# Loading both token pairs ahead of the value weights in a gated linear-attention and MLP kernel, with new engine orders

## The chip, the cores and the metric

The kernel runs on one core of a Trainium2 chip (trn2). The metric is device time in microseconds (us) of one execution. A core has five engines that each work through their own list of instructions: TensorE (PE in the profile, with its weight loads listed as PEld), VectorE (DVE), ScalarE (ACT), GpSimd (POOL) and SyncE (SP), which here only issues DMAs. ScalarE issues the stores of the output.

## The reference

Inputs are 2048 tokens `x` of 512 bf16 values, and weights in bf16. Two branches are computed and mixed by a gate for each token:

```python
g = sigmoid((x * gate_w).sum(-1, keepdims=True))
# branch a: linear attention with 32 heads of 16
q, k, v = split(x @ wqkv)                       # wqkv is 512 x 1536
pq, pk = q @ w_phi[h], k @ w_phi[h]             # 16 x 16 for each head
phi = concat([softmax(p), softmax(-p)])         # of pq and of pk, 32 features a head
kv = sum over tokens of phi_k (x) v;   z = sum over tokens of phi_k
a = ((phi_q @ kv) / (phi_q @ z + 1e-6)) @ wo
# branch b: MLP
b = relu(x @ w1) @ w2                           # 512 -> 1376 -> 512
out = g * a + (1 - g) * b
```

The sums `kv` and `z` run over all tokens, so no output of branch a can be formed before the key features of the last token tile are in them.

## The kernel before

Tokens are handled in 16 tiles of 128 (index m) and in 4 chunks of 512 (index c). The program is a graph of named tasks. Each task has an engine, a function that emits its instructions and a list of tasks it depends on. The order of the tasks on each engine is not found at run time: it is written out in the table `ORDER`, one list of names for each engine (lines 17 to 63). An engine works strictly in that order and, ahead of a task, waits on semaphores for those of its dependencies that lie on other engines or are DMAs. The numbers `dur` and `lat` in the task definitions are planning figures; they emit nothing.

The tasks that matter here, with the lines of the profile:

- `xa0`, `xa1` (L265): DMAs on SP's queue that bring the first 512 tokens into `XN` (part of the buffer `FT`), two tiles in each. A partition receives two neighbouring rows from each DMA, 2 KB in one piece.
- `wva`, `wvb` (L265): the value weights, two halves of 256 rows, 1 KB a row. `w1a`, `w1b`, `w1c` bring `w1`, `wphi` the 16 x 16 matrices, `wkT` and `wqT` (L269) the key and query weights by transposing DMA, `x1` to `x3` the other three chunks of tokens, transposed by DMA.
- `xt0a` to `xt3b` (L325): the "turns", which transpose the first four token tiles on TensorE, two 128 x 128 blocks in each task (a and b). `xe00` to `xe31` move the results into `XT`, the a half on ScalarE (L337), the b half on VectorE (L339).
- `warm0`, `warm1` (L251): matmuls on constants at the start.
- `v0a` to `v3b` (L374): the values of the first four tiles, in half tasks of two matmuls; half a needs `wva`, half b `wvb`. `v4` to `v15` are whole, four matmuls. `ve0` to `ve15` (L379, ScalarE) move them to `VS`.
- `f1_j` and `f0_j` (L356): the fold of the key and query weights with the 16 x 16 matrices, laid out as block-diagonal `WBD` (`wbd0` to `wbd3`, VectorE, L309, made from `wphi`). `fe1_0`, `fe1_2` (VectorE, L319), `fe1_1`, `fe1_3` (ScalarE, L317) move the folded key weights to `WP`.
- `pr_k0` to `pr_k8`, `pr_q0` to `pr_q8` (L454): projections with the folded weights, two tiles a task (the last two tasks of each kind one tile). They share PSUM banks 0 and 1, so each waits for the eviction (`ev_`, L479, ScalarE) of the one before.
- The features of a projection, for each J in k0 to q8: `mx_J`, `mn_J` (VectorE, L483, L485: maximum and minimum of each head), `t1_J`, `t2_J` (GpSimd, L492: the subtractions), `ex_J` (ScalarE, L497), `sm_J` and `rc_J` (VectorE), `nm_J` (GpSimd, L506 for k, L529 for q: the normalisation).
- `kv0` to `kv15` (L513): the sums of key features by values. `kn`, `kz` (VectorE) take the sums out of PSUM behind `kv15`, and `nd` (L556), the numerators and denominators, need these.
- `h c_k` (L397) and `hr c` (L405): the MLP's first layer, `rl` (L415) its ReLU; three PSUM banks in turn. `b m` (L577) the second layer, `a m` (L583) the output projection into the same bank, `oe m` (L628) the gated eviction and `st m` (L631) the store. `gt` and `gv` fold the gate's weight into `w1`.

The first tasks in the lists before, of SP and of TensorE:

```python
"sp": "xa0 wva xa1 wvb w1a wphi wkT w1b x1 gw w1c wqT x2 x3 w2a w2b ..."
"pe": "warm0 xt0a xt0b xt1a xt1b v0a v1a xt2a xt2b xt3a xt3b warm1 v2a v3a v0b v1b v2b v3b h0_0 f1_0 f1_1 f1_2 "
      "f1_3 h0_1 pr_k0 h0_3 h0_2 pr_k1 h0_6 h0_4 pr_k2 h0_5 h0_7 pr_k3 ..."
```

Of the kernel before, what the change touches and what calls it, by code (L numbers as in the profile page):

```python
# [18 lines left out]
        "xa0 wva xa1 wvb w1a wphi wkT w1b x1 gw w1c wqT x2 x3 w2a w2b ht1 wo ht0 tq1 tq0 tq2 tq3 to0 to1 ht2 to2 "  # L19
        "tq4 tq5 to3 tq6 tq7 to4 to5 ht3 tq8 tq9 to6 to7 tq11 tq10 to8 to9 tq12 tq13 to11 to10 tq14 tq15 to12 "  # L20
# [18 lines left out]
    ),  # L39
    "dve": (  # L40
# [10 lines left out]
    ),  # L51
# [91 lines left out]
def bass_gated_mix__linear_kernel_hedgehog__dense_activation_relu__prompt_kernel(  # L143
# [11 lines left out]
    x2 = A_x.rearrange("b s d -> (b s) d")  # L155
    o2 = out.rearrange("b s d -> (b s) d")
    S, D = x2.shape
# [23 lines left out]
    with ExitStack() as es:  # L181
# [67 lines left out]
        def pe_warm(q, sizes):  # L249
            for n in sizes:  # L250
                last = q.matmul(PS[:, 5, 0:n], ONE[:, 0:P], ONE[:, 0:n], start=True, stop=True)  # L251
            return last

        add("warm0", "pe", lambda q: pe_warm(q, (D, D, D, D, D, D, P)), (), dur=1.36)
        add("warm1", "pe", lambda q: pe_warm(q, (2 * P,)), (), dur=0.108)
# [21 lines left out]
        def pair(i):  # L277
            return x2[2 * i * P:2 * (i + 1) * P, :].rearrange("(p t) d -> p (t d)", t=2)

        load("xa0", "sp", XN[:, 0:2, :].rearrange("p t d -> p (t d)"), pair(0), dur=0.47, lat=2.25)  # L280
        load("wva", "sp", WV[:, 0:2, :], wvr[:, 0:2, :], dur=0.46, lat=2.55)
        load("xa1", "sp", XN[:, 2:4, :].rearrange("p t d -> p (t d)"), pair(1), dur=0.5, lat=3.2)
        load("wvb", "sp", WV[:, 2:4, :], wvr[:, 2:4, :], dur=0.48, lat=3.75)
        load("w1a", "sp", W1[:, :, 0:512], w1r[:, :, 0:512], dur=0.51, lat=4.75)
        load("wphi", "sp", WPS[:, :, :], A_w_phi.rearrange("(g hl) r c -> (hl r) g c", g=ND), dur=0.55, lat=4.4)
        load_t("wkT", WT[:, ND:2 * ND, :], A_wqkv[:, D:2 * D], (), 4.1, 2.1)
# [61 lines left out]
        def rows(m):  # L348
            if m < 4:
                i = m // 2  # L350
                return o2[2 * i * P:2 * (i + 1) * P, :].rearrange("(p t) d -> p t d", t=2)[:, m % 2, :]
            return o2[m * P:(m + 1) * P, :]
# [30 lines left out]
        for m in range(4):  # L383
            for n, js in enumerate(((0, 1), (2, 3))):
                add(f"v{m}{'ab'[n]}", "pe", lambda q, m=m, js=js: pe_v(q, m, js, VB[m]),
                    (f"xe{m}{n}", f"wv{'ab'[n]}", *(("warm1",) if m == 3 else ()), *((f"v{m}a",) if n else ())), dur=0.44)
            evict_v(m, VB[m], (f"v{m}b",))
# [246 lines left out]
        for line in (("warm0", "xt0a", "xt0b", "xt1a", "xt1b", "v0a", "v1a", "xt2a", "xt2b", "xt3a", "xt3b", "warm1",  # L634
                      "v2a", "v3a", "v0b", "v1b", "v2b", "v3b", "h0_0"),
                     ("xe00", "xe10", "xe20", "xe30", "ve0"),
                     ("ident", "xe01", "xe11", "xe21", "xe31", "shift", "blk", "row4", "mk", "wbd0"),
                     ("iota_r", "iota_i", "iota_c", "gwz", "pads", "ones")):
            for a, b in zip(line, line[1:]):
                g.follow(a, b)  # L640
# [39 lines left out]
```

## Time and profile before

| | us |
|---|---|
| median of 3 runs (151.42 to 151.90) | 151.71 |
| the profiled execution | 151.17 |
| its span, first to last instruction | 149.2 |
| TensorE busy | 144.9 |
| VectorE busy | 110.8 |
| GpSimd busy | 109.7 |
| ScalarE busy | 91.1 |

The profile shows one execution. Its span leaves out 1.97 us that lie around the first and last instruction. Busy times are of matmuls, vector operations and so on; waiting and issuing of DMAs are not counted. Where a line of the profile gives a start and a length, both are in us from the start of the span; "[0.50 <-DMA WT...]" behind a line is the idle time of that engine just before, and what ended it. In the rows of DMA traffic, "under 2 KB" counts all packets smaller than that, those under 512 B included.

### The profile page before, as it was taken

Reading aid. Unit: us, or ns where it says so; the run is one execution under the profiler, and the core shown is the slowest. Engines: PE = TensorE matmul, PEld = TensorE weight load, DVE = VectorE, ACT = ScalarE, POOL = GpSimd, SP = SyncE. Lnnn points to the kernel's source line nnn. Section 1 sums busy time; section 2 is a strip of 40 time slices with the busy share of each in tenths; the row PEclk is TensorE's granted clock in tenths of the full one; section 3 lists DMA queues with packets and bytes.
Section 4 is the critical chain, followed back from the end, with each engine's and each line's share of the span. In section 5 each row is a group of like instructions: output and inputs, shape, how many; then the busy total and the mean of one; then the engine's idle time right before and its main releaser. Section 6 shows DMA issues by size and latency. Waiting matters only on the chain.

```text
span 149.2 us, 2538 instructions
## 1 busy us (share of the span) xinstructions
PE 144.9 (97%) x968; PEld 73.0 (49%) x984; DVE 110.8 (74%) x169; ACT 91.1 (61%) x127; POOL 109.7 (74%) x73
## 2 busy tenths in 40 slices
PE   7899999999999999999999999999999999999994
PEld 2454444454454645444547445444545454544553
DVE  0542679999995499989569899999979987817501
ACT  3347769997886888966896854476535443303131
POOL 4000599999999999999999999999958795060000
PEclk9999999999999999999999999999999999999999
DMA  5999999500003400000000061847495964787423
GB/s 140 295 199 223 259 166 276 191 0 0 4 2 94 116 7 0 0 0 0 4 0 0 0 141 32 151 104 186 102 172 109 245 156 107 135 208 211 106 73 108
DMA packets 45524, 16.11 MB, mean 108 GB/s; under 512 B 39272, under 2 KB 45256, under 8 KB 45512
## 3 DMA queue, kind: packets, MB, share of 16 engines
q1 hardware_dynamic: 43208, 13.89, 42.3%
q10 hardware_dynamic: 2304, 2.06, 4.3%
q8 instruction: 8, 0.13, 0.4%
q14 instruction: 4, 0.03, 0.1%
HBM read 4.41 MB, written 2.10 MB: 44 GB/s over the span
## 4 chain that ended last, share of the span: by engine, by line
PE 94%; DMA 3%; issue 1%; SPq 1%; DVE 0%
PE PS L577 24%; PE PS L397 23%; PE PS L454 19%; PE PS L374 9%; PE PS L583 9%; PE PS L513 3%; DMA FT<-in_A_x_dram 3%; PE PS L556 3%; PE PS L405 2%; PE PS L598 2%; PE PS L356 1%; PE PS L609 1%; SPq L265 1%; PE PS L325 0%; DVE OSB L619 0%
## 5 line engine op out<-in xcount | busy, mean ns | idle before, releaser
L492 POOL TENSOR_TENSOR TS<-PB,MX 128x1024 bf16<-128x1024 bf16 (+1 forms) x18 | 30.8, 1716 | 13.9 <-DVE MX L483 13.9
L499 DVE TENSOR_REDUCE ZB<-FT 128x128 f32<-128x2048 bf16 (+1 forms) x18 | 36.6, 2037 | 4.6 <-ACT FT L497 4.5
L397 PE MATMUL PS<-XT,W 128*128 128x512 bf16 x155 | 37.7, 379 | 0.3
L577 PE MATMUL PS<-W,HT 128*128 128x512 bf16 (+1 forms) x161 | 37.0, 379 | 0.2
L497 ACT ACTIVATE FT<-TS 128x2048 bf16<-128x2048 bf16 (+1 forms) x18 | 31.0, 1720 | 4.5 <-PE PS L513 2.4
L492 POOL TENSOR_TENSOR TS<-MN,PB 128x1024 bf16<-128x1024 bf16 (+1 forms) x18 | 30.8, 1720 | 0.1
L454 PE MATMUL PS<-WP,XT 128*128 128x512 bf16 x126 | 30.1, 379 | 0.1
L506 POOL TENSOR_TENSOR FT<-FT,SC 128x2048 bf16<-128x2048 bf16 (+1 forms) x9 | 29.5, 3285 | 0.0
L415 ACT ACTIVATE HT<-PS 128x512 bf16<-128x512 f32 x40 | 22.8, 601 | 6.3 <-PE PS L397 6.2
L628 ACT ACTIVATE OSB<-PS,OMG 128x512 bf16<-128x512 f32 x15 | 10.2, 685 | 23.5 <-PE PS L583 23.5
L479 ACT ACTIVATE PB<-PS 128x1024 bf16<-128x1024 f32 (+1 forms) x18 | 16.8, 932 | 12.3 <-PE PS L454 8.1
L577 PEld LDWEIGHTS PS<-W,HT 128*128 128x128 bf16 (+1 forms) x165 | 15.5, 97 | 17.4 <-ACT OSB L628 0.3
L397 PEld LDWEIGHTS PS<-XT,W 128*128 128x128 bf16 x160 | 15.0, 98 | 17.5 <-ACT HT L415 1.0
L483 DVE TENSOR_REDUCE MX<-PB 128x64 bf16<-128x1024 bf16 (+1 forms) x18 | 19.5, 1082 | 5.4 <-ACT PB L479 5.4
L485 DVE TENSOR_REDUCE MN<-PB 128x64 bf16<-128x1024 bf16 (+1 forms) x18 | 19.2, 1075 | 0.3 <-ACT PB L479 0.2
L454 PEld LDWEIGHTS PS<-WP,XT 128*128 128x128 bf16 x128 | 12.1, 98 | 14.0 <-DVE WP L319 0.4
L529 POOL TENSOR_TENSOR FT<-FT,SR 128x1024 bf16<-128x1024 bf16 (+1 forms) x9 | 15.6, 1736 | 0.6
L374 PE MATMUL PS<-WV,XT 128*128 128x512 bf16 x61 | 15.5, 379 | 0.2
L583 PE MATMUL PS<-WO,OT 128*128 128x512 bf16 x58 | 14.4, 378 | 0.1
L564 DVE SCALAR_TENSOR_TENSOR OTM<-PS,EG,RD 128x256 bf16<-128x256 f32 x32 | 14.1, 466 | 0.4
L562 DVE RECIPROCAL RD<-PS 128x16 f32<-128x16 f32 x32 | 7.0, 238 | 8.2 <-PE PS L556 7.9
L379 ACT ACTIVATE VS<-PS 128x512 bf16<-128x512 f32 x16 | 9.5, 607 | 3.0 <-PE PS L374 3.0
(54 smaller groups left out, 96.3 us busy)
## 6 DMA issues: line engine op xcount, KB each, us to landing
out_dram<-OSB ACTq DMA_DIRECT2D x15, 128.0 KB, 2.5
W<-in_B_w_dram SPq DMA_DIRECT2D x1, 1280.0 KB, 8.2
W<-in_B_w_dram SPq DMA_DIRECT2D x2, 512.0 KB, 5.0
FT<-in_A_x_dram SPq DMA_DIRECT2D x2, 256.0 KB, 3.4
WV<-in_A_wqkv_dram SPq DMA_DIRECT2D x2, 256.0 KB, 3.7
WO<-in_A_wo_dram SPq DMA_DIRECT2D x1, 512.0 KB, 4.6
W<-in_B_w_dram SPq DMA_DIRECT2D x1, 352.0 KB, 3.6
PHQ<-FT SPq DMA_TRANSPOSE x16, 2.8
```

What stands on the lines that cost most here:

```text
L374: last = q.matmul(PS[:, b, :], XT[:, j, m * P:(m + 1) * P], WV[:, j, :], start=(j == 0), stop=(j == ND - 1))
L397: last = q.matmul(PS[:, b, :], W1[:, j, k * P:(k + 1) * P], XT[:, j, chunk(c)], start=(j == 0), stop=(j == ND - 1))
L415: add(f"rl{a}_{k}", "act", lambda q, a=a, k=k, b=b: q.activation(HT[:, k, chunk(a)], PS[:, b, :], ACT.Relu), (f"h{a}_{k}",), dur=0.6)
L454: last = q.matmul(PS[:, n, :], XT[:, j, m * P:(m + 1) * P], WP[:, s, j, :], start=(j == 0), stop=(j == ND - 1))
L483: add(f"mx_{J}", "dve", lambda q, sl=sl, w=w, i=pbg: q.tensor_reduce(MX[:, sl, 0:w * H], i, AX.X, ALU.max), (f"ev_{J}", old("t1")), dur=0. ...
L485: add(f"mn_{J}", "dve", lambda q, sl=sl, w=w, i=pbg: q.tensor_reduce(MN[:, sl, 0:w * H], i, AX.X, ALU.min), (f"ev_{J}", old("t2")), dur=0. ...
L492: add(f"{tn}_{J}", "pool", lambda q, o3=o3, a3=a3, b3=b3: q.tensor_tensor(o3, a3, b3, ALU.subtract), (f"{'mx' if sg == 0 else 'mn'}_{J}", ...
L497: add(f"ex_{J}", "act", lambda q, fs=fs, ts=ts, w=w: q.activation(FT[:, fs, 0:w * F], TS[:, ts, 0:w * F], ACT.Exp), (f"t1_{J}", f"t2_{J}", ...
L499: add(f"sm_{J}", "dve", lambda q, fs=fs, sl=sl, w=w: q.tensor_reduce(ZB[:, sl, 0:2 * w * H], FT[:, fs, 0:w * F].rearrange("p (g d) -> p g ...
L506: add(f"nm_{J}", "pool", lambda q, f3=f3, sl=sl, w=w: q.tensor_tensor(f3, f3, SC[:, sl, 0:2 * w * H].unsqueeze(2).to_broadcast([P, 2 * w * ...
L577: last = q.matmul(PS[:, ab, :], HT[0:r, k, m * P:(m + 1) * P], W2[0:r, k, :], start=(k == 0), stop=False)
L583: last = q.matmul(PS[:, ab, :], OT[:, m % NOT, t, :], WO[:, t, :], start=False, stop=(t == ND - 1))
```

## The change

The DMAs of SP are put in the order xa0, xa1, wva, wvb. The first 512 tokens are laid out anew: a partition now holds four neighbouring rows, of which xa0 brings the first two and xa1 the other two, so that both read from the same 512 KB of `x` in pieces of 2 KB every 4 KB. The stores of tiles 0 to 3 follow this layout. `warm1` is taken out. On TensorE the written rule that binds the first tasks now asks only for the turns in order and then `h0_0`; the list itself has all turns but `xt3a` and `xt3b` ahead of the values. The lists of all engines are new; the set of tasks is the same but for `warm1`. In the changed kernel the lines below the table stand one to three higher (L265 is L264, L356 is L353).

```diff
     "sp": (
-        "xa0 wva xa1 wvb w1a wphi wkT w1b x1 gw w1c wqT x2 x3 w2a w2b ht1 wo ht0 tq1 tq0 tq2 tq3 to0 to1 ht2 to2 "
+        "xa0 xa1 wva wvb w1a wphi wkT w1b x1 gw w1c wqT x2 x3 w2a w2b ht0 ht1 wo tq1 tq0 ht2 tq2 tq3 to0 to1 tq4 "
...
     "pool": (
-        "iota_r iota_i iota_c gwz pads ones t1_k0 t2_k0 t1_k1 t2_k1 t1_k2 t2_k2 nm_k0 t1_k3 t2_k3 t2_k4 t1_k5 "
-        "t1_k4 nm_k2 nm_k1 t2_k5 t2_k6 t1_k6 nm_k3 t1_k8 t1_k7 t2_k7 t2_k8 nm_k4 t2_q0 t1_q0 nm_k5 t1_q1 t2_q1 "
-        "nm_k6 t1_q2 ra_q0 t2_q2 nm_q0 nm_k7 nm_k8 ra_q1 nm_q1 t1_q3 t2_q3 t1_q4 ra_q2 nm_q2 t2_q4 t2_q5 ra_q3 "
...
+        "iota_r iota_i iota_c gwz pads ones t1_k0 t2_k0 t1_k1 t2_k1 t2_k2 t1_k2 t2_k3 t1_k3 t1_k4 nm_k0 t2_k4 "
+        "nm_k1 t1_k5 t2_k5 nm_k2 t2_k7 t1_k6 t2_k6 t1_k7 nm_k3 t2_q0 t1_k8 nm_k4 t2_k8 t1_q0 nm_k5 nm_k6 t2_q1 "
+        "t1_q1 ra_q0 t2_q2 nm_q0 t1_q2 nm_k7 nm_k8 ra_q1 nm_q1 t1_q3 t2_q3 ra_q2 nm_q2 t1_q4 t2_q4 t1_q5 ra_q3 "
...
     "act": (
-        "xe00 xe10 xe20 xe30 ve1 ve2 ve3 fe1_1 fe1_3 ve0 rl0_0 ev_k0 rl0_3 rl0_1 rl0_2 ev_k1 rl0_6 rl0_4 ev_k2 "
-        "ex_k0 rl0_5 ev_k3 rl0_9 ex_k1 rl0_8 ev_k4 ex_k2 rl1_0 rl0_7 rl1_1 ev_k5 rr0 ve4 ex_k3 ev_k6 rl1_4 rl1_2 "
...
+        "xe00 xe10 xe20 xe30 ve1 ve2 rl0_0 fe1_1 fe1_3 rl0_3 rl0_1 ve0 ev_k0 ve3 rl0_6 ev_k1 rl0_2 ev_k2 ex_k0 "
+        "rl0_5 ev_k3 rl0_4 ex_k1 rl0_9 ev_k4 ve4 rl0_8 ex_k2 rl0_7 ev_k5 ve5 ex_k3 rl1_0 rl1_1 ve6 ev_k6 rl1_3 "
...
     "dve": (
-        "ident xe01 xe11 xe21 xe31 shift blk wbd3 wbd2 row4 mk wbd1 wbd0 fe1_0 fe1_2 mx_k0 mn_k0 mx_k1 mn_k1 "
-        "mx_k2 mn_k2 sm_k0 rc_k0 mx_k3 mn_k3 mx_k4 gv mn_k4 sm_k2 mx_k5 gr0 sm_k1 rc_k2 sm_k3 mx_k6 rc_k1 mn_k5 "
...
+        "ident xe01 xe11 xe21 xe31 shift blk row4 wbd2 wbd1 mk wbd3 wbd0 fe1_2 fe1_0 mx_k0 mn_k0 mx_k1 mn_k1 gv "
+        "mx_k2 mn_k2 sm_k0 mn_k3 mx_k3 mx_k4 mn_k4 rc_k0 sm_k2 sm_k1 mx_k5 rc_k1 mn_k6 gr0 rc_k2 mn_k5 sm_k3 "
...
     "pe": (
-        "warm0 xt0a xt0b xt1a xt1b v0a v1a xt2a xt2b xt3a xt3b warm1 v2a v3a v0b v1b v2b v3b h0_0 f1_0 f1_1 f1_2 "
-        "f1_3 h0_1 pr_k0 h0_3 h0_2 pr_k1 h0_6 h0_4 pr_k2 h0_5 h0_7 pr_k3 h0_9 h0_8 pr_k4 h1_1 h1_0 gt pr_k5 v4 "
-        "hr0 h1_3 pr_k6 v5 kv0 h1_4 h1_2 pr_k7 h1_7 v6 h1_5 hr1 v7 h1_8 v8 f0_0 h1_6 v9 h1_9 pr_k8 kv1 f0_3 v10 "
...
-        "h3_2 h3_9 h3_5 b2 kv14 h3_8 kv15 b1 nd0_1 nd1_0 nd0_0 pr_q6 nd1_1 b0 nd2_1 nd2_0 pr_q7 nd3_0 a0 nd3_1 "
...
+        "warm0 xt0a xt0b xt1a xt1b xt2a xt2b v1a xt3a v0a v1b xt3b v2a v2b v0b v3a h0_0 h0_1 f1_2 f1_1 f1_0 f1_3 "
+        "h0_3 pr_k0 h0_6 v3b pr_k1 h0_2 gt pr_k2 h0_5 h0_4 pr_k3 v4 h0_9 pr_k4 h0_7 h0_8 pr_k5 v5 h1_1 hr0 h1_0 "
+        "v6 pr_k6 h1_3 v7 h1_4 pr_k7 kv0 h1_7 kv1 h1_2 h1_6 pr_k8 hr1 v8 h1_5 h1_9 h1_8 kv2 f0_1 v9 f0_2 f0_0 "
...
+        "h3_7 h3_5 hr3 b1 kv14 h3_8 kv15 pr_q6 nd0_1 nd0_0 b2 nd1_0 nd1_1 b0 nd2_1 nd2_0 pr_q7 a0 nd3_0 nd3_1 a1 "
...
-        add("warm1", "pe", lambda q: pe_warm(q, (2 * P,)), (), dur=0.108)
...
-        def pair(i):
-            return x2[2 * i * P:2 * (i + 1) * P, :].rearrange("(p t) d -> p (t d)", t=2)
-
-        load("xa0", "sp", XN[:, 0:2, :].rearrange("p t d -> p (t d)"), pair(0), dur=0.47, lat=2.25)
-        load("wva", "sp", WV[:, 0:2, :], wvr[:, 0:2, :], dur=0.46, lat=2.55)
-        load("xa1", "sp", XN[:, 2:4, :].rearrange("p t d -> p (t d)"), pair(1), dur=0.5, lat=3.2)
-        load("wvb", "sp", WV[:, 2:4, :], wvr[:, 2:4, :], dur=0.48, lat=3.75)
+        first = x2[0:4 * P, :].rearrange("(p t) d -> p t d", t=4)
+        for i in range(2):
+            load(f"xa{i}", "sp", XN[:, 2 * i:2 * i + 2, :].rearrange("p t d -> p (t d)"),
+                 first[:, 2 * i:2 * i + 2, :].rearrange("p t d -> p (t d)"), dur=0.47, lat=2.4 + 0.1 * i)
+        load("wva", "sp", WV[:, 0:2, :], wvr[:, 0:2, :], dur=0.48, lat=2.8)
+        load("wvb", "sp", WV[:, 2:4, :], wvr[:, 2:4, :], dur=0.5, lat=3.2)
...
             if m < 4:
-                i = m // 2
-                return o2[2 * i * P:2 * (i + 1) * P, :].rearrange("(p t) d -> p t d", t=2)[:, m % 2, :]
+                return o2[0:4 * P, :].rearrange("(p t) d -> p t d", t=4)[:, m, :]
...
-        for line in (("warm0", "xt0a", "xt0b", "xt1a", "xt1b", "v0a", "v1a", "xt2a", "xt2b", "xt3a", "xt3b", "warm1",
-                      "v2a", "v3a", "v0b", "v1b", "v2b", "v3b", "h0_0"),
+        for line in (("warm0", "xt0a", "xt0b", "xt1a", "xt1b", "xt2a", "xt2b", "xt3a", "xt3b", "h0_0"),
```

More of the change, by code (lines that the diff above doesn't have):

```diff
@@ L18 @@
     "sp": (
-        "xa0 wva xa1 wvb w1a wphi wkT w1b x1 gw w1c wqT x2 x3 w2a w2b ht1 wo ht0 tq1 tq0 tq2 tq3 to0 to1 ht2 to2 "
-        "tq4 tq5 to3 tq6 tq7 to4 to5 ht3 tq8 tq9 to6 to7 tq11 tq10 to8 to9 tq12 tq13 to11 to10 tq14 tq15 to12 "
+        "xa0 xa1 wva wvb w1a wphi wkT w1b x1 gw w1c wqT x2 x3 w2a w2b ht0 ht1 wo tq1 tq0 ht2 tq2 tq3 to0 to1 tq4 "
+        "tq5 to2 to3 tq6 tq7 to4 to5 ht3 tq8 to6 tq9 to7 tq10 tq11 to8 tq13 tq12 to9 to10 tq14 to11 tq15 to12 "
         "to13 to14 to15 st15_1 "
@@ L276, in bass_gated_mix__linear_kernel_hedgehog__dense_activation_relu__prompt_kernel @@
         wvr = A_wqkv[:, 2 * D:3 * D].rearrange("(j p) n -> p j n", p=P)
-        def pair(i):
-            return x2[2 * i * P:2 * (i + 1) * P, :].rearrange("(p t) d -> p (t d)", t=2)
-        load("xa0", "sp", XN[:, 0:2, :].rearrange("p t d -> p (t d)"), pair(0), dur=0.47, lat=2.25)
-        load("wva", "sp", WV[:, 0:2, :], wvr[:, 0:2, :], dur=0.46, lat=2.55)
-        load("xa1", "sp", XN[:, 2:4, :].rearrange("p t d -> p (t d)"), pair(1), dur=0.5, lat=3.2)
-        load("wvb", "sp", WV[:, 2:4, :], wvr[:, 2:4, :], dur=0.48, lat=3.75)
+        first = x2[0:4 * P, :].rearrange("(p t) d -> p t d", t=4)
[4 more added lines that the diff above has]
+        load("wvb", "sp", WV[:, 2:4, :], wvr[:, 2:4, :], dur=0.5, lat=3.2)
         load("w1a", "sp", W1[:, :, 0:512], w1r[:, :, 0:512], dur=0.51, lat=4.75)
         load("wphi", "sp", WPS[:, :, :], A_w_phi.rearrange("(g hl) r c -> (hl r) g c", g=ND), dur=0.55, lat=4.4)
-        load_t("wkT", WT[:, ND:2 * ND, :], A_wqkv[:, D:2 * D], (), 4.1, 2.1)
+        load_t("wkT", WT[:, ND:2 * ND, :], A_wqkv[:, D:2 * D], (), 4.3, 2.0)
         load("w1b", "sp", W1[:, :, 512:1024], w1r[:, :, 512:1024], dur=0.61, lat=4.0)
@@ L385, in bass_gated_mix__linear_kernel_hedgehog__dense_activation_relu__prompt_kernel @@
                 add(f"v{m}{'ab'[n]}", "pe", lambda q, m=m, js=js: pe_v(q, m, js, VB[m]),
-                    (f"xe{m}{n}", f"wv{'ab'[n]}", *(("warm1",) if m == 3 else ()), *((f"v{m}a",) if n else ())), dur=0.44)
+                    (f"xe{m}{n}", f"wv{'ab'[n]}", *((f"v{m}a",) if n else ())), dur=0.44)
             evict_v(m, VB[m], (f"v{m}b",))
```

40 rows, old and new, of the table ORDER are left out of this document.

## The prediction

> **What bounds the kernel now.** First the busy shares and the granted clock on the page: TensorE is at work for nearly the whole span, at full clock in every slice.
>
> ```profile
> PE 144.9 (97%) x968; PEld 73.0 (49%) x984; DVE 110.8 (74%) x169; ACT 91.1 (61%) x127; POOL 109.7 (74%) x73
> PEclk9999999999999999999999999999999999999999
> ```
>
> Then the chain of waits in order of time over the first 14 us (start, length, what):
>
> ```profile
> 1.67 4.13 DMA FT<-in_A_x_dram
> ...
> 5.85 0.62 PE PS L325 x8
> ...
> 6.61 2.76 PE PS L374 x12
> ...
> 10.25 1.07 PE PS L356 x16
> ```
>
> The second pair of tokens (xa1, third on SP's queue) lands at 1.67 + 4.13 = 5.80; its turns, then twelve of the sixteen matmuls of v0 to v3, h0_0 and the fold f1 follow. Next the DMA view by half microseconds, from 2.5, 3.0, 3.5, 4.0, 4.5 and 5.0 us:
>
> ```profile
> DMA packets 119, 0.18 MB, mean 365 GB/s; under 512 B 10, under 2 KB 50, under 8 KB 119
> DMA packets 185, 0.18 MB, mean 369 GB/s; under 512 B 7, under 2 KB 183, under 8 KB 185
> DMA packets 84, 0.10 MB, mean 201 GB/s; under 512 B 15, under 2 KB 55, under 8 KB 84
> DMA packets 53, 0.09 MB, mean 170 GB/s; under 512 B 7, under 2 KB 16, under 8 KB 53
> DMA packets 105, 0.14 MB, mean 276 GB/s; under 512 B 1, under 2 KB 74, under 8 KB 105
> DMA packets 154, 0.17 MB, mean 348 GB/s; under 512 B 15, under 2 KB 123, under 8 KB 154
> ```
>
> Packets of 2 KB are tokens, of 1 KB weights. The rate dips as xa1 begins: its 128 packets spread over 3.5 to 5.5 us (29, 37, 31, 31). Against 365 GB/s the dip loses 0.082 + 0.098 + 0.045 = 0.22 MB, or 0.6 us.
>
> Then the timeline, for what follows the transposed key weights (wkT, issued 3.71, 6.5 us to landing: 10.2), and the waits of GpSimd:
>
> ```profile
> 10.25 0.90 PEld L356 LDWEIGHTS PS<-WBD,WT 128*128 128x128 bf16 x16 [0.50 <-DMA WT<-in_A_wqkv_dram]
> 12.11 1.42 PEld L454 LDWEIGHTS PS<-WP,XT 128*128 128x128 bf16 x8 [0.42 <-DVE WP L319]
> 16.42 1.91 POOL L492 TENSOR_TENSOR TS<-PB,MX 128x1024 bf16<-128x1024 bf16 x1 [13.95 <-DVE MX L483]
> ```
>
> ```profile
> POOL TS L492 <- DVE MX L483: 13.9, 1, 13.9
> POOL SR L525 <- DVE SC L523: 7.9, 3, 4.9
> ```
>
> wkT releases f1, f1's evictions release pr_k0, and 6.17 us after f1 starts GpSimd starts t1_k0. After that it runs back to back past 89 us (the 7.9 us on L525 come later than 109). Last, what that means at 89 us, where kv15, the final matmul of the key-value sums, waits for nm_k8 on GpSimd:
>
> ```profile
> 85.53 3.83 POOL L506 TENSOR_TENSOR FT<-FT,SC 128x1024 bf16<-128x1024 bf16 x2
> 88.64 1.02 PE L397 MATMUL PS<-XT,W 128*128 128x512 bf16 x4
> 89.40 0.40 PEld L513 LDWEIGHTS PS<-VS,FT 128*128 128x128 bf16 x8 [0.23 <-POOL FT L506]
> 89.50 0.42 PE L513 MATMUL PS<-VS,FT 128*128 128x65 bf16 x8
> ```
>
> nm_k8 ends at 89.36, kv15's first weights load at 89.40, and its first matmul at 89.50 is just where h3_8 is out (88.64 + 4 x 0.216). TensorE and GpSimd arrive together: TensorE has no margin to be early. From there to its last matmul it runs without a gap. So the end is set by whichever is later at kv15, and GpSimd's side is f1's start plus 79.1 us.
>
> **The change, part by part.** *Loads.* xa1 moves ahead of wva. xa0 keeps first place and lands at 0.74 + 2.7 = 3.4. Second place landed at 1.21 + 3.0 = 4.2 and third at 5.8. If the dip goes, third place is 786 KB: about 0.475 MB had moved by 3.5 us, the other 0.311 MB at 365 GB/s takes 0.85, so 4.35, and the two loads ahead landed 0.4 to 0.5 after their bytes: 4.8 for wva, and 0.7 more, 5.5, for wvb. If the dip stays, 5.8 and 6.5, third and fourth place of now. Why should it go? Before, xa0 and xa1 read two separate 256 KB blocks of the tokens, and the dip starts with the first packets of the second block; with four neighbouring rows to a partition both loads read the same 512 KB, and xa0 has been to every 4 KB piece. WV's blocks, though, begin without a dip, so this is an inference. I take 4.85. No row shows tokens read 2 KB in every 4; the bounds are those two cases. The stores of tiles 0 to 3 keep their 1 KB rows, 4 KB apart instead of 2; they are issued from 101.45 to 115.86 us, land in 2.5 to 3.2, and their buffers are taken again only eight tiles later: nothing.
>
> *wkT.* It is seventh on SP as before, issued at about 3.7. Packets under 512 B (wphi's and its own) begin only when the loads ahead have drained (229 of them from 6.5 to 7.0 us), so its landing should follow the drain: 10.2 less up to 0.6. Bounds: 10.2 and 9.6; I take 9.6 to 9.8, which is then covered by TensorE (below). If that fails, see B.
>
> *TensorE's head.* warm1 goes: 0.11 us that lay in the wait until 6.61 for the eviction xe20, so nothing. All turns but xt3a and xt3b now stand ahead of v1a; they end near 4.65, in the wait for wva. Then, until f1: seven half tiles of v (2 x 0.216 each, 3.02), xt3a and xt3b (0.11 each, from eight matmuls in 5.85 to 6.3), h0_0 and h0_1 (0.863 each), and 0.05 from landing to start: f1 at wva + 5.02. Their other inputs are early: xe20 comes from xt2a at 4.5, wvb is needed only at wva + 1.0, and w1a (2.65 + 5.5 = 8.15 at the latest) at 8.15. With 4.85: 9.87, against 10.25. wphi's landing (3.16 + 5.3 = 8.5) and the block weights made from it by 9.7 still fit.
>
> *From f1 to GpSimd.* f1_2 comes first, on VectorE; two evictions on each engine as now (1.29 and 1.09), h0_3 under them where h0_1 was: still 6.17. GpSimd starts 0.38 earlier.
>
> *TensorE's body.* At f1 it is ahead by h0_1 less v3b, 0.43. But pr_k2 now follows pr_k1 behind h0_2 and gt alone, 0.89 us, and needs ev_k1: the row for pr_k1 (15.59 + 1.73 = 17.32) to its eviction (17.51 + 1.02) asks for 1.24 with the next start, so 0.35 is given back. pr_k1 has 1.29 (h0_6, v3b), just enough. Now f1 to kv15 takes 89.50 - 10.25 = 79.25, of which 0.11 is a wait at pr_k0 (for f1's evictions) and 0.09 one at f0_0 (v8 is out at 44.02 + 0.86 = 44.88, f0_0 starts at 44.97). The new order holds 0.43 less, keeps the first wait, has more room ahead of the first fold and adds 0.35: 79.25 - 0.43 - 0.09 + 0.35 = 79.08. With f1 at 10.25 TensorE would be at kv15 at 89.33, 0.17 before it can run it, and waits. Behind kv15 the same matmuls follow as now. v3b's eviction ve3 (0.6) now comes at 15.3 and is still out before h0_2 needs its bank at 16.9.
>
> *GpSimd's order.* The set ahead of nm_k8 is the same, so its 73 us are. New is t2_k3 in seventh place, due at 27.66 where mn_k3 ended only at 29.8. The earlier pr_k2 pays for this: ev_k2 by 21.1, ex_k0 22.9, sm_k0 (2.04) 25.5, mn_k3 26.6: 1.0 to spare.
>
> **Sum.** The gain is that of f1's start, 0.38 us: 149.2 - 0.4 = 148.8 of span; the profiled execution took 151.17, 1.97 more than its span, so 150.8. That run was 0.54 below the median of 151.71; on the median, 151.35. A difference under 0.3% (0.46 us), about what a measurement of this kernel can tell from no change, is "same".
>
> **The rivals.**
>
> A, the forecast (0.44): f1 between 9.7 and 10.1, time 151.15 to 151.55. Two in five of it, with some luck in the medians, falls beyond 0.46.
>
> B (0.15): the dip goes, wkT does not follow and stays at 10.2. For it: SP's own issue of it lasts 4.44 us, to 8.15, and may set the pace. Then f1 is at 10.25 and GpSimd as now; the 0.43 us of extra work done early is spent on pr_k2 and at kv15. 151.7: the title's edit works and nothing is won.
>
> C, slower (0.23): the dip comes with the time or the place in the queue, not with the token block, and now falls on wva, 5.8. f1 at 10.82, GpSimd 0.57 later: 152.3. For it: the dip begins at 3.5 us, about when SP starts the transposed load (3.71). Against: every byte ahead of it is now of one region or of weights, which ran at 365. It decides at wva = 5.2: later than that, f1 is later than 10.25. The cause is one: v0a and v1a, once run at 4.40 with the second load in place, have none of their weights until the third is in.
>
> D, the clock (0.05): between the turns (4.65) and v1a TensorE idles 0.2 to 1.2 us, and warm1 is gone. The first matmuls of 512 columns started 0.43 apart, later ones 0.216; full speed came 2.76 us after the first. If the wait drops it again for that long, half of 2.76 is lost: 1.4 on top of C, near 153.5, or 152.7 without. Against: the 0.42 wait ahead of 5.85 cost nothing, the next matmuls came at 0.216.
> The Trainium skill, "TensorE: Matmul & The Clock Gate", Part 1 (The HAM clock gate), puts the fall after about 3.4 us of idling and the window as free-running; by that rule a wait of 1.2 us leaves the clock alone, and the 0.42 us wait here agrees; no run so far shows a longer one.
>
> E (0.10): a hole in GpSimd's row at one of the reordered features, t2_k3 first: each us that mn_k3 is later than 1.0 past my walk is a us of the end; 0.5 to 1 us: 151.9 to 152.4.
>
> The last 0.03: my margin at kv15 is wrong and TensorE's whole lead counts, 151.0.
>
> **How the numbers follow.** Faster: two fifths of A, the last case, and a little of B by scatter: 0.18 + 0.03 + 0.05 = 0.26. Slower: two thirds of C, D, most of E, a little of B: 0.15 + 0.05 + 0.08 + 0.05 = 0.33. Same: 0.41. The range leaves out most of D and the far end of E: 150.9 to 152.5.
>
> **What would show it.** Right: the half-microsecond DMA rows from 3.5 to 5.0 near 365 GB/s; the first WV load landed by 4.9, 3.2 after its issue; L353 (f1's new line) starting at 9.8 to 9.9; a wait near 0.35 us ahead of the matmuls of pr_k2; GpSimd's first L489 at 16.0 with no idle time to kv15; kv15's weights waiting for GpSimd. Wrong: f1 held by wkT at 10.2 (B); token or WV rows at 170 to 200 GB/s (C); matmuls of 512 columns 0.43 apart after 4.9 us (D); idle time of L489 on GpSimd (E); or an end that moves with TensorE though GpSimd's start does not.

## The result: slower by 1.3%, and the profile after

The changed kernel takes 153.06 us (median of six executions, 152.41 to 154.63), against 151.56 for the kernel before, timed beside it: a ratio of 1.0133, 95% interval 1.0100 to 1.0166. The forecast was 151.35 with a range up to 152.5, so the result lies outside, on the slow side. The profiled execution took 152.83 us with a span of 151.0; before it was 151.17 and 149.2. So 1.8 us have to be found in the trace. The ratios here leave out five executions, of 220, 258 and 874 us and of 153.63 (to9_first) and 157.19 us (lead), the last two over 1.5% above the fastest of their kernel.

The busy share first. TensorE does the same work as before, 144.8 us, in a longer span: the 1.8 us are idle time. Two slices of the 40 show it: the 35th stands at 7 tenths instead of 9, and the second at 7 instead of 8.

```profile
PE   7899999999999999999999999999999999999994
```

```profile
PE   7799999999999999999999999999999999799994
PEclk9999999999999999999999999999999999999999
```

The first row is of the kernel before, the other two of the changed one.

Then the chain of waits over the first 16 us (start, length, what):

```profile
1.67 4.19 DMA WV<-in_A_wqkv_dram
5.86 0.14 issue
5.99 0.59 PE PS L371 x2
...
9.40 1.73 PE PS L394 x8
11.12 0.89 PE PS L353 x16
```

The third load on SP's queue is now wva, and it lands at 1.67 + 4.19 = 5.86; before, the third was xa1, at 5.80. TensorE stands still from 4.94 until 5.99, and the fold f1 begins at 10.96 instead of 10.25. GpSimd follows it with the old distance, 6.16 us (start, length, engine, and idle time before it):

```profile
10.96 1.06 PE L353 MATMUL PS<-WBD,WT 128*128 128x128 bf16 x16
17.12 1.91 POOL L489 TENSOR_TENSOR TS<-PB,MX 128x1024 bf16<-128x1024 bf16 x1 [14.65 <-DVE MX L480]
```

From there GpSimd runs back to back to nm_k8, and kv15 waits for that as it did:

```profile
90.03 0.35 PEld L510 LDWEIGHTS PS<-VS,FT 128*128 128x128 bf16 x8 [0.27 <-POOL FT L503]
90.09 0.42 PE L510 MATMUL PS<-VS,FT 128*128 128x65 bf16 x8
```

kv15 starts 0.59 us later than before (90.09 against 89.50). That accounts for a third of the loss. The rest comes behind kv15. From TensorE's waits (total, how often, longest):

```profile
PE PS L580 <- DMA OT<-OTM: 1.1, 1, 1.1
PE PS L371 <- DMA WV<-in_A_wqkv_dram: 1.0, 1, 1.0
```

The second of these is the wait for wva. The first is new, and in the kernel before there was no wait behind kv15 at all. It is at a9, whose input to9 is a transposing DMA (`tq` and `to` are SyncE's transposes of the query features, PHQ, and of branch a's rows, OT). The timeline shows the wait, and SyncE's issues ahead of it:

```profile
132.03 1.04 PE L580 MATMUL PS<-WO,OT 128*128 128x512 bf16 x4 [1.07 <-DMA OT<-OTM]
...
121.38 1.21 SPq L566 DMA_TRANSPOSE OT<-OTM  x1
123.15 2.66 SPq L529 DMA_TRANSPOSE PHQ<-FT  x2
125.86 3.93 SPq L566 DMA_TRANSPOSE OT<-OTM  x2
```

These are to8, then tq13 and tq12, then to9 and to10. to9's input, o9_1, was ready at 123.67, but SyncE reaches to9 only at 125.86, behind the two tq. It lands 6.12 us later, at 131.98, where the median of its kind on the page is 2.4. In the kernel before the list read to8 to9 tq12 tq13, and to9, issued at 123.39, landed at 127.80, for a start of a9 at 127.85. The views of before (the first line is to8 and to9, the second tq12 and tq13, the last a9):

```profile
121.61 2.97 SPq L569 DMA_TRANSPOSE OT<-OTM  x2
125.42 3.17 SPq L532 DMA_TRANSPOSE PHQ<-FT  x2
...
127.85 1.04 PE L583 MATMUL PS<-WO,OT 128*128 128x512 bf16 x4
```

That transfer had no margin, and the prediction did not look at it. On TensorE's new list a9 stands behind b11 instead of ahead of it, so to9 now had until 130.96, the end of b11; it came 4.18 us later than before.

Why 6.12? The DMA view by single microseconds, 126 to 127 (first two lines), 127 to 128 and 129 to 130 (last line):

```profile
DMA packets 508, 0.15 MB, mean 146 GB/s; under 512 B 507, under 2 KB 507, under 8 KB 507
q8 instruction: 1, 0.02, 10.1%
...
DMA packets 3, 0.00 MB, mean 1 GB/s; under 512 B 3, under 2 KB 3, under 8 KB 3
...
q14 instruction: 1, 0.01, 1.9%
```

A packet of 16 KB of instructions (queue q8) begins at 126.33 and takes 1.6 us; behind it the 256-byte packets of the transposes stand nearly still, from 126.8 to 128.7. Twenty-one of these packets, begun between 126.52 and 126.79, took up to 2.23 us each, where their kind mostly takes 0.018. A second packet of instructions, of 8 KB on queue q14, comes at 129.07, and 19 packets begun from 129.50 to 129.56 took 0.8 to 0.9 us each. The three transposes under way at the first packet, tq13, tq12 and to9, landed 5.70, 6.07 and 6.12 us after their issue; of the other 25 tq and to with no 16 KB packet in their flight the median is 2.8 and the longest 3.7. Eight packets of 16 KB occur in every run of these kernels, here from 17.9 to 146.3 us. Before, one at 125.57 fell into the flight of to9 itself: fifteen of its 16 DMA engines were done by 126.36, the last at 127.80. So the missing margin of the kernel before goes with such a packet as well.

The last matmul ends at 148.82 instead of 147.02, 1.81 later: 0.59 up to kv15 and 1.22 behind it.

### The profile page after: what moved, and what is told of

Read it like the earlier page. It is cut to its first block, busy times and chain, and to the rows that moved or that the text cites. A ratio compares the mean times of both kernels' runs of the same rounds, so it can differ in the third digit from the quotient of the medians.

```text
span 151.0 us, 2539 instructions
## 1 busy us (share of the span) xinstructions
PE 144.8 (96%) x966; PEld 73.2 (48%) x983; DVE 110.4 (73%) x169; ACT 91.7 (61%) x127; POOL 109.7 (73%) x73
## 3 DMA queue, kind: packets, MB, share of 16 engines
HBM read 4.41 MB, written 2.10 MB: 43 GB/s over the span
## 4 chain that ended last, share of the span: by engine, by line
PE 85%; DMA 7%; DVE 4%; issue 2%; ACT 1%; SPq 1%
PE PS L394 22%; PE PS L574 18%; PE PS L451 17%; PE PS L371 9%; PE PS L580 8%; DMA OT<-OTM 4%; PE PS L510 3%; DMA WV<-in_A_wqkv_dram 3%; PE PS L553 2%; PE PS L402 2%; PE PS L595 2%; DVE ZB L496 1%; PE PS L353 1%; ACT PB L476 1%; DVE OTM L561 1%
## 5 line engine op out<-in xcount | busy, mean ns | idle before, releaser
L574 PE MATMUL PS<-W,HT 128*128 128x512 bf16 (+1 forms) x161 | 37.5, 379 | 0.2
L412 ACT ACTIVATE HT<-PS 128x512 bf16<-128x512 f32 x40 | 23.3, 597 | 8.8 <-PE PS L394 8.8
L559 DVE RECIPROCAL RD<-PS 128x16 f32<-128x16 f32 x32 | 6.3, 229 | 8.6 <-PE PS L553 8.6
```

Source lines behind the costliest of these rows:

```text
L412: add(f"rl{a}_{k}", "act", lambda q, a=a, k=k, b=b: q.activation(HT[:, k, chunk(a)], PS[:, b, :], ACT.Relu), (f"h{a}_{k}",), dur=0.6)
L574: last = q.matmul(PS[:, ab, :], HT[0:r, k, m * P:(m + 1) * P], W2[0:r, k, :], start=(k == 0), stop=False)
```

## Experiments

Each time is a median; the ratio is to the kernel before, timed on the same chip in the same call (151.36, 151.63, 151.42 and 151.41 us in the four calls).

**The list: to9 back in front.** Theory Q says that the wait at a9 comes from to9's place on SyncE's list.

```diff
-to8 tq13 tq12 to9 to10     (the changed kernel)
+to8 to9 tq13 tq12 to10
```

> The changed kernel with one move on SyncE's list: to9 stands ahead of tq13 and tq12, as it did before the change. Theory Q (the change lost 0.6 us at its head and 1.1 us where a9 waits for to9, because SyncE issues to9 only behind tq13 and tq12, whose inputs come later, and these are held up on the way): to9 is issued by 125 us and lands by 127.5, a9 follows b11 without a gap, the kernel is 0.8 to 1.2 us faster than the changed one, about 0.5 us (0.3%) slower than the one before. Rival S (the transposing DMAs near 127 us are slow whatever their order, so the wait moves to a10 or to the tokens' numerators that need tq12): to9 is in time, but a10 or nd12_0 waits 0.8 to 1.2 us and the time stays at the changed kernel's, 1.2 to 1.3% over the one before.

Measured: 152.05 us, ratio 1.0047 (1.0015 to 1.0080). The wait at a9 is gone: to9 lands at 127.91, a9 starts at 132.51. By the starts and ends of the tasks 0.29 us for to10 are left. Later profiles agree: where to9 stands behind the two tq, a9 waits 0.67 us (wva_second) and 1.25 (pairs_back); in the five further kernels of the new lists with to9 in front it does not wait. In rows_only, which has the old lists, it waits 0.18, so close was the margin before. The twelve executions here lie in two stretches, six from 151.28 to 151.81 and six from 152.29 to 153.63. The profile fell on one of the upper six (153.43), and its head shows why that one is late:

```profile
5.86 1.01 PE L371 MATMUL PS<-WV,XT 128*128 128x512 bf16 x2 [0.72 <-DMA WV<-in_A_wqkv_dram]
...
6.87 1.91 PE L371 MATMUL PS<-WV,XT 128*128 128x512 bf16 x4
```

Four matmuls of 512 columns take 1.91 us, 0.43 apart; in the changed kernel's own profile four of them take 1.03, 0.216 apart. Half speed lasts here until 9.65, and f1 starts at 12.68, 1.7 us later than there, although the page's row of granted clock shows 9 in all slices. The other five were not profiled.

**The list alone, in the kernel before.**

```diff
-to8 to9 tq12 tq13          (the kernel before)
+to8 tq12 tq13 to9
```

> The kernel before with one part of the change alone: on SyncE's list to9 goes behind tq12 and tq13 (to8 tq12 tq13 to9 instead of to8 to9 tq12 tq13). Theory Q (to9 waits on SyncE behind two transposes that a fetch of instructions has slowed, and a9 waits for it): to9 lands 131 to 132 instead of 127.8, TensorE waits 0.8 to 3 us for it at a9, most likely 1.2 to 1.9 since a9 comes 0.6 earlier here than in the changed kernel; 152.4 to 153.2 us, f1 stays at 10.2 to 10.3. Rival (the wait at a9 comes with the late start at f1 and not with the list): no wait at a9 over 0.3, 151.3 to 151.8.

> The kernel before with to9 behind tq12 and tq13 on SyncE's list once more, for a profile of an ordinary execution (the six times of it were 154.86 to 156.73 and one of 220.29, which the profile fell on). Theory Q with the measured 156.3: TensorE waits about 4 to 5 us for to9 at a9, which lands only at 131 to 133, and the rest stays as in the kernel before. Rival (a wait elsewhere, or a slower clock in many executions): a9 waits under 2 us and other waits or matmuls of half speed make up the rest.

Measured: 156.44 us (156.29 without the execution of 220 us; ratio 1.0306, 1.0271 to 1.0341) and, in two executions, 156.87 (1.0352, 1.0295 to 1.0410). One name moved by two places costs about 5 us. The second run's profile shows where:

```profile
PEclk9999999999999999999999999999999999599999
...
121.70 1.22 SPq L569 DMA_TRANSPOSE OT<-OTM  x1
125.51 2.98 SPq L532 DMA_TRANSPOSE PHQ<-FT  x2
128.54 3.89 SPq L569 DMA_TRANSPOSE OT<-OTM  x3
...
131.38 1.79 PE L583 MATMUL PS<-WO,OT 128*128 128x512 bf16 x4 [3.22 <-DMA OT<-OTM]
132.96 5.89 PE L577 MATMUL PS<-W,HT 128*128 128x512 bf16 x21
```

SyncE stands at tq12 from 122.92 to 125.51, because that waits for nm_q6 on GpSimd; to9, whose input was ready at 123.38 in the kernel before, is behind it and is issued at 128.54. Up to there f1 (10.33) and kv15 stand within 0.1 us of the kernel before. It lands at 131.33, and TensorE waits 3.22 us, over the 0.8 to 3 of the first expectation and under the 4 to 5 of the second. Then comes what neither theory had expected: after this wait the clock falls, to 5 in one slice of the row above. By windows (the stretch, its length, the busy time and count of PE, PEld, DVE, ACT and POOL, then the granted clock, the DMAs' busy share and GB/s):

```profile
126.00:130.00 4.00, 2.16 (x21) 1.10 (x18) 3.56 (x8) 0.69 (x1) 0.00 (x0) 1.00 0.70 143
130.00:134.00 4.00, 2.62 (x7) 1.03 (x8) 0.56 (x3) 0.69 (x1) 2.58 (x4) 0.69 0.52 104
134.00:136.00 2.00, 1.86 (x8) 0.79 (x7) 0.00 (x0) 0.00 (x0) 0.00 (x0) 0.77 1.12 276
136.00:152.00 16.00, 15.95 (x116) 8.73 (x115) 5.19 (x17) 3.33 (x6) 0.00 (x0) 1.00 0.34 96
```

The clock lost 4 x 0.31 + 2 x 0.23 = 1.7 us, which is 3.4 us at half speed. So 3.22 of waiting and 1.7 of clock make 4.9 of the 5.2 us by which the last matmul is late (152.24 against 147.02). The Trainium skill, "TensorE: Matmul & The Clock Gate", Part 1 (The HAM clock gate), puts the fall after an idle window of about 3.4 us and the return after a busy one of the same length. The 3.4 us at half speed agree, and so does the 1.07 us wait of the changed kernel, which left the clock at 1.00 (130 to 134 us). The idle time ahead of the fall is 3.22 us from the modelled end of the matmul before and 3.41 from its start, too near the figure of the Trainium skill to tell.

**The fetch.** Redundant waits, always already met, add 90 instructions to TensorE's list in the layers h of chunks 1 to 3, so that the instruction packets fall at other places of the work.

```diff
             for j in range(ND):
+                if c and j:
+                    for n in (three of the long finished loads):
+                        q.wait_ge(sems[n], 16)
                 last = q.matmul(PS[:, b, :], W1[:, j, k * P:(k + 1) * P], XT[:, j, chunk(c)],
```

> The changed kernel, its lists untouched, with 90 further instructions on TensorE that change nothing: waits on loads that have long landed, three of them together ahead of a matmul in the first layer of chunks 1 to 3. Theory F (an instruction fetch of 16 KB, which comes with every 256 or so instructions of TensorE and lies at 126 to 128 us in each trace, holds up the transposing DMAs then under way, tq13, tq12 and to9, for 1 to 2 us): the fetch comes about 6 us earlier, near 120, the held packets with it, to9 lands before 130 and the wait of a9 goes: 0.7 to 1.2 us faster than the changed kernel, 0.2 to 0.6% over the one before. Rival N (the transposes near 127 us are slow for what is queued there): the fetch moves, the wait stays at 1 us or more and so does the time. If the added waits cost TensorE time themselves, its gaps show it and the wait of a9 is read from the trace.

Measured: 152.91 us, ratio 1.0109 (1.0057 to 1.0161). The packet that fell at 126.33 now falls at 123.69, and the one before it at 102.92 instead of 108.4. There it finds another transpose with little margin, to2 for a2 (0.4 us in the changed kernel):

```profile
107.12 1.04 PE L583 MATMUL PS<-WO,OT 128*128 128x512 bf16 x4 [1.61 <-DMA OT<-OTM]
...
101.76 3.82 SPq L569 DMA_TRANSPOSE OT<-OTM  x2
```

That issue took 2.51 in the changed kernel, and to2 lands at 107.08 instead of 104.89. Up to there the run keeps to the changed kernel (kv15 at 90.12 and 90.09). So here the shifted packet alone makes a transpose late enough to stall TensorE.

At a9 the run says less. The wait is gone with the list unchanged, but to9 lands at 131.91, as late as in the changed kernel (131.98), and theory F had asked for less than 130. After the wait at a2 all is later: b11 starts 1.80 us later (130.22 against 128.42), and to9 is issued 1.86 later, at 127.72. What shrank is its flight, to 4.18 us from 6.12; that is more than the 1.07 of the wait, but with no 16 KB packet under way 4.18 is still over the 2.4 of its kind, so other traffic, the 8 KB packet at 129.18 for one, slows it too (rival N in part). By an estimate from the changed kernel's own rows, to9 issued at 125.86 with a flight of 2.4 would have landed at 128.3, ahead of the end of b11 at 130.96. So the wait at a9 needs two things together: the list, which to9_first shows, and a slow flight, for which the instruction packets are the likely but not the isolated cause. The loss moved and did not shrink.

**The loads: place, layout or content?** In the prediction the dip in the DMA rate went with the two-row layout (theory L); its rival C had it go with time or place in the queue. Three kernels separate these: wva second in the changed kernel; the four-row layout alone in the kernel before; the two-row layout put back in the changed kernel.

```diff
-xa0 xa1 wva wvb            (wva_second: loads, in the changed kernel)
+xa0 wva xa1 wvb
-xt2a xt2b v1a xt3a v0a v1b xt3b v2a     (and TensorE's list)
+v0a v1a xt2a xt2b xt3a xt3b v2a v1b
```

> The changed kernel with the old place of wva: SyncE's order is xa0, wva, xa1, wvb again (with the four-row layout), and TensorE runs v0a and v1a behind the first four turns as it did before; all other lists stay new. Theory Q: wva lands near 4.2, xa1 between 5.2 and 5.9, the fold f1 starts at 9.9 to 10.5 where the changed kernel has 10.96, so the head's loss goes: 0.4 to 0.7 us faster than the changed kernel, with the wait of a9 still there (about 1 us, 0.7 to 0.8% over the one before). Rival H (the wait of a9 is only a consequence of the late head, by which an instruction fetch meets other transposes): both go, and the kernel is within 0.2% of the one before.

```diff
-            return x2[2 * i * P:2 * (i + 1) * P, :].rearrange("(p t) d -> p (t d)", t=2)
+            return x2[0:4 * P, :].rearrange("(p t) d -> p t d", t=4)[:, 2 * i:2 * i + 2, :]...
```

> The kernel before with the four-row layout alone: all lists, the order of the loads and warm1 as before; only which rows a partition holds, and the stores of tiles 0 to 3, change. Theory L of the prediction (the dip in the DMA rate from 3.5 to 5 us comes from xa1 being the first to touch a second block of the tokens, and goes with the layout): the 2 KB packets of xa1 go at 300 GB/s or more, xa1 lands between 4.9 and 5.3 where it was 5.8, the kernel is 0.1 to 0.4 us faster, limited by the key weights. Rival T (the dip belongs to the third place in the queue, or to the moment): xa1 lands at 5.7 to 5.9 with the rate near 200 GB/s from 3.5 to 4.5, time equal to the one before within 0.2%.

```diff
-                 first[:, 2 * i:2 * i + 2, :].rearrange("p t d -> p (t d)"), ...
+                 x2[2 * i * P:2 * (i + 1) * P, :].rearrange("(p t) d -> p (t d)", t=2), ...
```

> The changed kernel with the old two-row layout: the loads stay in the new order xa0, xa1, wva, wvb, all lists new. Theory L (the layout keeps the rate up): the dip comes back, now on xa1 in second place, wva lands at 6.0 to 6.6 and the kernel is 0.2 to 0.7 us slower than the changed one. Rival T (layout does not matter): wva lands at 5.5 to 6.0 as in the changed kernel, and the time is the changed kernel's within 0.2%, 1.1 to 1.5% over the one before.

| kernel | second lands | third lands | f1 starts | us | ratio (95%) |
|---|---|---|---|---|---|
| before | wva 4.18 | xa1 5.81 | 10.25 | 151.56 | 1 |
| after | xa1 4.50 | wva 5.86 | 10.96 | 153.06 | 1.0133 (1.0100 to 1.0166) |
| wva_second | wva 4.21 | xa1 6.08 | 10.92 | 152.51 | 1.0082 (1.0059 to 1.0104) |
| rows_only | wva 4.41 | xa1 6.28 | 10.96 | 151.80 | 1.0031 (1.0019 to 1.0043) |
| pairs_back | xa1 4.11 | wva 5.86 | 10.96 | 152.73 | 1.0081 (1.0065 to 1.0097) |

The third load lands at 5.8 to 6.3 whichever layout it has and whatever it carries, and the second lands early either way. Theory L falls. In pairs_back the second block of tokens is first touched by the second load, and that one lands at 4.11 (its time, 0.81% over, lies below the 1.1 to 1.5% that rival T gave). The dip itself is still there in the changed kernel, half a microsecond earlier, over weights and tokens of the new layout alike. By half microseconds from 3.0, 3.5, 4.0, 4.5 and 5.0:

```profile
DMA packets 77, 0.13 MB, mean 260 GB/s; under 512 B 11, under 2 KB 16, under 8 KB 77
DMA packets 76, 0.09 MB, mean 176 GB/s; under 512 B 5, under 2 KB 61, under 8 KB 76
DMA packets 130, 0.13 MB, mean 258 GB/s; under 512 B 6, under 2 KB 128, under 8 KB 130
DMA packets 139, 0.13 MB, mean 268 GB/s; under 512 B 8, under 2 KB 139, under 8 KB 139
DMA packets 183, 0.18 MB, mean 352 GB/s; under 512 B 11, under 2 KB 183, under 8 KB 183
```

The trace's record of landings shows what a landing is: each load is shared out over 16 DMA engines, 13 of which were done with wva by 5.17, the last three between 5.72 and 5.86. The Trainium skill, "DMA: Bandwidth & Descriptors", section "Why a DMA increments its semaphore by 16 and not by 1", says that only all sixteen mean a landing; the trace agrees, as v1a starts at 5.99, behind the last of them.

The place of wva alone does not bring the head back. Theory Q asked for f1 at 9.9 to 10.5 in wva_second; it starts at 10.92. The third load is then xa1, at 6.08, and the first matmuls run at half speed (see below). Besides, TensorE's new list has h0_1 (0.86 us) ahead of f1 where the old one had the half task v3b (0.43), so 0.43 us more work lies there, wherever wva stands.

The four rows may even cost: rows_only is 0.31% slower, beyond the 0.2% of rival T, and xa1 as the third load landed at 6.08 and 6.28 with four rows (wva_second and rows_only), at 5.81 in the kernel before. Each landing is of a single profile, so this is not shown.

**Is it the transposed load behind it?** SP starts to issue wkT at 3.71, in the middle of the dip. In this kernel (with to9 in front) w1b goes ahead of it.

```diff
-wvb w1a wphi wkT w1b x1
+wvb w1a w1b wphi wkT x1
```

> The changed kernel with to9 ahead of tq13 and tq12, and with w1b ahead of wphi and wkT on SyncE's queue, so that the first transposing DMA is issued near 4.3 us where it was 3.7. One look at the landing of the third load. Theory X (issuing the transposing DMA at 3.7 us is what holds some of the 16 rings of the third load, so that it lands at 5.7 to 6.3 in all six profiles, whatever it brings): wva lands by 5.2. Rival Y (the third load lands late for its place in the queue alone): wva lands at 5.7 to 6.2 again. The whole time is no measure here, since the key weights come later by 1 us or more.

Measured, in a single execution with a profile: 152.49 us. wkT is issued at 4.28, and wva, third, still lands at 5.74; from 3.5 to 4.0 the DMAs move 98 GB/s. The transposed load is not what holds the third one back. wkT lands at 11.7, and f1 waits 0.74 for it.

**The clock in the head.** Two matmuls of 512 columns on constants fill the wait for wva (with to9 in front).

```diff
-xt2a xt2b v1a xt3a
+xt2a xt2b warm1 v1a xt3a
```

> The changed kernel with to9 ahead of tq13 and tq12, and two matmuls of 512 columns on constants in TensorE's wait for wva (between xt2b and v1a). Theory K (the spread of the changed kernel's times is TensorE's clock: in half of the executions the idle stretch of 1 us ahead of v1a leaves the matmuls at half speed until about 9 us, and the start costs 1.7 us more; the profile of to9_first shows it, 0.427 us a matmul from 5.86 to 8.8): with the wait filled the slow half goes, all times lie within 0.8 us of each other near 151.3 to 151.8, median 0.4 to 0.8 us under to9_first. Rival V (the spread comes from the landing of the loads or from the DMAs near 127 us): the spread stays at 2 us and the median near 152.0.

Measured: 151.60 us, ratio 1.0016 (0.9993 to 1.0039). Of the eleven executions nine lie from 151.20 to 151.75 and two at 152.5; without the filler it was six and six. That speaks for the idle time as a cause of the half-speed heads, but does not show it: wva_second and rows_only ran their first four matmuls of v at half speed (1.89 and 1.76 us for four) from 4.4 and 4.5 on, before the long wait of this order could come. Eleven executions against twelve are few, too. The profile fell on one of the two at 152.5: its matmuls run at full speed from 6.42 on, and f1 is late, at 11.55, because wvb landed only at 7.42 and TensorE waited 0.53 us for it. So the landing of the loads spreads the times as well, as rival V had it.

**Both repairs, and two attempts at a better kernel.** "both" has to9 in front and wva second.

> The changed kernel with to9 ahead of tq13 and tq12, and with wva back in second place (v0a and v1a run behind the first four turns). Theory Q (two independent losses, the head by the place of wva and the wait of a9 by SyncE's order, and in the head a share for the clock): within 0.3% of the kernel before, 151.2 to 151.8, without a wait of a9 over 0.3 us. Rival E (the new lists themselves cost, by pr_k2's wait or elsewhere): still 0.4% or more over the one before, with other waits on TensorE than pr_k0 and pr_k2 in sum over 0.5 us.

Measured: 151.72 us, ratio 1.0014 (0.9994 to 1.0034), twelve executions from 151.25 to 152.07, no second group. In its profile TensorE waits for nothing over 0.3 us after f1 but the 0.39 at pr_k2. It is back at the time of the kernel before, not ahead of it. In the profile kv15 still starts 0.67 us later than before (90.17), as f1 does 0.79 later (11.04, with xa1 at 6.34), so the head's loss is still there; the times show at most 0.5 of this. The two profiles exaggerate it: that of the kernel before fell on an execution 0.39 us under its median (151.17 of 151.56), that of "both" on one 0.19 over (151.91).

"lead" puts wkT ahead of w1a in it and f1 ahead of all h; "lead2" puts wphi and wkT ahead of w1a. ScalarE's first tasks follow in both (not printed).

```diff
-wvb w1a wphi wkT w1b                                       (both)
+wvb wkT w1a wphi w1b                                       (lead)
+wvb wphi wkT w1a w1b                                       (lead2)
-v0b v3a h0_0 h0_1 f1_2 f1_1 f1_0 f1_3 h0_3 pr_k0 h0_6 v3b pr_k1 h0_2 gt pr_k2
+v0b v3a v3b f1_2 f1_1 f1_0 f1_3 h0_0 pr_k0 h0_1 h0_3 pr_k1 h0_6 h0_2 gt pr_k2       (lead)
+v0b v3a f1_2 f1_1 f1_0 f1_3 v3b pr_k0 h0_0 h0_1 pr_k1 h0_3 h0_6 gt pr_k2            (lead2)
```

> The changed kernel with to9 back in front of tq13 and tq12 and wva loaded second, and besides: wkT ahead of w1a on SyncE, f1 ahead of the first h, all eight half turns of v ahead of f1, one h more ahead of pr_k2. If the start of GpSimd's row sets the end: f1 starts at about 9.8 instead of 11.04 and all ends about 1.2 earlier, 150.4 to 150.7 us against 151.6 for the kernel before. If TensorE's own row sets it: only the wait at pr_k2 (0.39) is gained, kv15 ends 0.3 to 0.5 earlier than in the kernel with both edits alone (90.61), 151.2 to 151.5 us. If w1a, now behind a transposing DMA, lands after 11: TensorE waits for it at h0_0 and the time is 151.8 to 152.5.

> The changed kernel with to9 back in front of tq13 and tq12 and wva loaded second, and besides: wphi and wkT ahead of w1a on SyncE (the attempt before left wphi behind, and f1 waited 3.5 us for WBD, which is made from it), f1 ahead of every h, one h more ahead of pr_k2. If the start of GpSimd's row sets the end: f1 starts at 8.7 to 9.3 instead of 11.04 and all ends 1.5 to 2 earlier, under 150.3 us. If TensorE's own row sets it: 0.2 to 0.6 are gained, 151.1 to 151.5 us. If w1a lands after 11.5 or later transposes come later, TensorE waits for them: 151.8 to 153.

Measured: lead 155.73 us (1.0264, 1.0228 to 1.0299), lead2 153.61 (1.0137, 1.0113 to 1.0160). Neither beats the kernel before. In lead the edit was at fault: f1 needs WBD, made from wphi, which now came later, and TensorE waits 3.5 us for it (its clock falls here too: the page's row reads 9995999). In lead2 f1 starts at 8.84 and GpSimd at 15.00, 2.2 us earlier than in "both", and yet kv15 is done 1.4 later, at 91.98. The early start was lost on waits in new places: of 1.44, 0.32 and 0.77 us on GpSimd (mn, mn, rc), and of 0.7 us twice on TensorE:

```profile
PE PS L395 <- ACT HT L413: 1.5, 2, 0.7
```

These are h0_6 and h0_5, whose banks are emptied by rl0_3 and rl0_2, and in my order these evictions came too late. So whether an early f1 pays under a matching order stays open.

## Why the prediction was wrong, point by point

**Loads: the step that failed first.** The third place was sized at 4.85 and measured 5.86, 1.01 late. The inference was that the dip belongs to a block of tokens touched for the first time, since it began with that block's packets; the experiments tie it to neither layout nor content nor to wkT's issue. The bound of 5.8 for "the dip stays" was right to 0.06. From there on rival C's chain held: 0.57 predicted at GpSimd and kv15; GpSimd started 0.70 later and kv15 0.59. Why the third load lands late stays open. C's chance of 0.23 was too low, given that the same load place had been seen at 5.80 and the reason for a change was, by the prediction's own words, an inference.

**"Behind kv15 the same matmuls follow as now": the step that failed second, and the larger term.** The matmuls are the same, in another order, but a9 waits 1.07 us for to9 and the stretch is 1.22 longer. The new SyncE list was in the change and its order was not costed; no rival covered it. to9_first, which puts that one name back, takes the wait away. Only with this term does the time leave the range: C alone gave 152.3. The two terms explain the whole miss: the span was forecast at 148.8 and measured 151.0, 2.2 more, of which 0.97 (0.38 of gain not had, 0.59 of loss) before kv15 and 1.22 behind it.

**The clock (D).** The execution profiled after the change runs its head at full speed, and so does not show D. But half-speed heads do occur, and cost about what D said: f1 1.7 us later in the profiled to9_first (D: 1.4). That the other five upper times there, and two of the changed kernel's own, 154.47 and 154.63, have the same cause is likely but was not profiled. D had 0.05. (By its own terms, 152.3 and 1.4, D on top of C is 153.7, not 153.5.)

**What held.** TensorE's head: wva to f1 5.10 (5.02 predicted). From f1 to GpSimd: 6.16 (6.17). pr_k2 waits 0.39 for ev_k1 (0.35). f1 to kv15: 79.13 (79.08). GpSimd's order: no idle time from t1_k0 to nm_k8, so E did not occur. Of the later holes there, that of 1.21 us ahead of t1_q8, at 124.33, is followed by no wait of TensorE's. One of 2.33 us, at 120.80, lies ahead of nm_q6, for which SyncE stands at tq13 until 123.15, with to9 behind it in the list. wkT landed at 10.00, between the bounds, and did not hold f1.

## What to carry to other kernels

Where a list of a DMA queue is rewritten, compare for every transfer its landing in the old trace with the start of its user: a margin of 0.05 us (to9 for a9) is a bound of the kernel, though no wait shows it, and one name moved behind two others there cost 5 us, with the fall of the clock behind the wait. A queue in order is held by the first task in it that is not ready, so look at what stands ahead, not only at when the input is done. And a landing time that goes with a place in the queue should be taken to stay with that place until a run shows otherwise.

## What the runs showed of the hardware

- The third load of 256 KB on SP's queue landed between 5.6 and 6.3 us in eleven of the kernels, at the end of its slowest DMA engines. The exceptions are lead and lead2, 5.08 and 5.38, where the 512 KB of w1a were not queued right behind wvb. That points to the loads behind as the cause; no run isolates it.
- An instruction packet of 16 KB took 0.9 to 1.8 us, and transposing packets of 256 B beside it took up to 2.23 us instead of 0.018; shifted onto another transpose, it stalled TensorE there for 1.61 us. With 90 more instructions on TensorE's list the later ones came 2 to 7 us earlier, so they go with the length of that list.
- The end of the half-speed phase in the head varies from one execution to the next, from about 4.4 to 9.65 us (by 6 in the changed kernel, which has the same program as to9_first up to to9), without a mark in the row of granted clock.
